# Routing operands in the unused half of the state's PSUM bank, the first expert's low parts subtracted on GpSimd, and x stored one chunk later

## The chip, the cores and the metric

The kernel runs on one core of a Trainium2 chip. Five engines work beside each other: TensorE (PE, with its weight load PEld), VectorE (DVE), ScalarE (ACT), GpSimd (POOL) and SyncE (SP), which here only issues transfers. Each engine takes its instructions in order. The metric is the device time of one execution in microseconds (us); lower is better.

## What is computed

A retention-like attention layer (B = 4 batches, 8 heads, 768 tokens, head size 64) feeds a mixture of 8 experts with two experts for each token.

```python
for t in range(S):
    state = gamma * state + einsum('bhd,bhe->bhde', k[:, :, t], v[:, :, t])
    y[:, :, t] = scale * einsum('bhd,bhde->bhe', q[:, :, t], state)
x = y.transpose(0, 2, 1, 3).reshape(B * S, H * D)            # 3072 x 512
noisy = x @ w_gate + log1p(exp(x @ w_noise)) * noise
top2 = argpartition(-noisy, 2, axis=1)[:, :2]
top2_w = softmax of the two                                 # with + 1e-9
for e in range(8):
    for k in range(2):
        mask = top2[:, k] == e
        h = maximum(x[mask] @ w1[e], 0)
        out[mask] += top2_w[mask, k, None] * (h @ w2[e])
```

## The kernel before

**Stages.** A loop over 24 chunks of 128 tokens (`for j in range(NCH)`, L672; six chunks, NC, make a batch) runs from the start to about 142 us: attention for chunk j, and in the same iterations the routing of batches that are complete and the preparation of the first expert's weights. From about 142 to 220 us the routing of the last batch and the token lists of all experts are finished while the first expert's products begin. From 220 to 690 us the eight experts run on TensorE.

**One iteration.** The order in which the code stands is the order on each engine. Iteration j has, in this order: `qk(j+1)` (L312: 16 products of k with the scaled q of the next chunk, into pA); `v_scale(j+1)` and `q_scale(j+2)` on GpSimd (L285, L291); loads for chunk j+4 on SP; `x_total(j-1)` (PE L348, sum of squares into XSS) and `x_hi(j-1)` (DVE L157 and L158 read XSS and make a power of two, `upx`; ACT L353 writes the fp16 high part of x); `masked(j+1)` (DVE L319); `x_lo(j-1)` (DVE L357, the low part); what the table `between` has for j; `y_mm(j)` (PE L326 and L329 into pY, ACT L334 squares it, PE L339 adds k v into the state's bank pU, ACT L345 copies the state to U in SBUF); `x_rows(j-2)` (PE L363 transposes, ACT L365 copies to `xr`, SP stores it to HBM, L366); `logits(j-2)` (PE L373 and L376 into PL); and at last what the table `todo` has for j. pU is written in columns 0 to 63 of each of its four 128-column parts; in the last chunk of a batch there is no state product. The buffers of `qs` number 3, of `vp`, `am` and pA 2 each, of pY 2.

**The routing.** When a batch is complete, its route steps run in the iterations that follow, with n the last iteration of the batch: `route_a` at n+2 (DVE L386 to L391 on the logits, ACT L394 and L395 Exp and Ln), `route_b` n+3 (L403 to L412: noise and the two best), `route_b2` and `route_c` n+4 (L419 one-hot rows, L422, L441, L442), `places` n+5 (PE L432, places within the experts, into POS), `route_d` n+5 (L465 to L487), `route_e` n+6 and n+7 (L498 and L500, 12 instructions each), `route_w` n+8 (gates), `table` n+8 (PE L506 into LST) and `route_f`. After batch 1 (iteration 19) three gathers of rows follow on GpSimd (L608). The routing of batches 0, 1 and 2 runs in iterations 7 to 13, 13 to 19 and 19 to 23.

**The first expert's weights.** Each of its two matrices comes in four pieces of 128x1024 fp32: `w_load` (SP), `w_sum` (ACT L181, sum of squares), `w_scale` (PE L184 into SUM, DVE: a power of two), `w_hi` (ACT L202, fp16 of the scaled piece), `w_lo` (DVE L207, scaled piece minus its high part, one instruction). The tables at L649 to L656 say in which iteration each stands. The other seven experts' weights are prepared in the stages behind, with the same functions.

**Banks and waits.** PSUM has eight banks here: pA (2), pY (2), pX, pU, pR and pL. Waits between engines are kept for each of these tiles as a whole: an engine that touches a tile waits for what another engine did with that tile before, whichever columns it was. XSS lies in pL beside the logits PL; POS, LST and SUM lie in pR.

Of the kernel before, what the change touches and what calls it, by code (L numbers as in the profile page):

```python
# [94 lines left out]
def moe_kernel(ctx, tc, qT, kT, kt, vt, noise, wgn, w1, w2, ctab, qtab, xbuf, gbuf, out):  # L95
# [35 lines left out]
    lanes = consts.tile([128, 128], F16, name="lanes")  # L131
    blks = consts.tile([128, NCOL], F16, name="blks")
# [6 lines left out]
    invx = consts.tile([128, NCH], F32, name="invx")  # L139
# [139 lines left out]
    VP, AM, QS, PY, X, SS = {}, {}, {}, {}, {}, {}  # L279
    pU = psum.tile([128, HP, 128], F32, name="pU")  # L280
# [78 lines left out]
    def x_rows(j):  # L359
# [6 lines left out]
        nc.sync.dma_start(xbuf[128 + j * C:128 + (j + 1) * C, :], xr)  # L366
# [13 lines left out]
    cum = work.tile([128, NL], F32, name="cum")  # L380
    nc.vector.memset(cum, 0.0)
    R["cum"] = cum

    def route_a(b):
        sl = slice(b * NC, (b + 1) * NC)
        nc.vector.tensor_scalar(invx[:, sl].bitcast(I32), upx[:, sl].bitcast(I32), -1.0, float(254 << 23),  # L386
# [637 lines left out]
```

## Time and profile before

| | |
|---|---|
| time, median of 3 runs (lowest, highest) | 705.52 us (703.36, 708.82) |
| profiled execution: its own time, its span | 706.42 us, 704.6 us |
| mean granted TensorE clock of that span | 0.972 |
| TensorE busy | 661.5 us (94%) |
| TensorE's weight load busy | 401.2 us (57%) |
| VectorE busy | 296.4 us (42%) |
| ScalarE busy | 315.0 us (45%) |
| GpSimd busy | 266.1 us (38%) |

The profile is of one execution. Its span is what the trace covers; the execution's own time is 706.42 - 704.6 = 1.8 us longer. Instructions are named by engine, line of the code, operation and tiles (`pL L373` is the instruction of line 373 that writes tile pL). "Busy" counts time in which an engine executes; overlapping instructions of a pipelined engine are counted once in a window. "PEclk" is the granted TensorE clock as a share of full speed (1.00 is 2.4 GHz, 0.50 is 1.2 GHz).

### The profile page before, as it was taken

Reading aid. Unit: us, or ns where it says so; the run is one execution under the profiler, and the core shown is the slowest. Engines: PE = TensorE matmul, PEld = TensorE weight load, DVE = VectorE, ACT = ScalarE, POOL = GpSimd, SP = SyncE. Lnnn points to the kernel's source line nnn. Section 1 sums busy time; section 2 is a strip of 40 time slices with the busy share of each in tenths; the row PEclk is TensorE's granted clock in tenths of the full one; section 3 lists DMA queues with packets and bytes.
Section 4 is the critical chain, followed back from the end, with each engine's and each line's share of the span. In section 5 each row is a group of like instructions: output and inputs, shape, how many; then the busy total and the mean of one; then the engine's idle time right before and its main releaser. Section 6 shows DMA issues by size and latency. Waiting matters only on the chain. (4 is left out here: it accounts for less than half of the span.)

```text
span 704.6 us, 12916 instructions
## 1 busy us (share of the span) xinstructions
PE 661.5 (94%) x5165; PEld 401.2 (57%) x5165; DVE 296.4 (42%) x800; ACT 315.0 (45%) x560; POOL 266.1 (38%) x214
## 2 busy tenths in 40 slices
PE   8997886989799999999999999999999999999992
PEld 5886775754576554555455545554654565455540
DVE  4678997868024534352215321522252144215100
ACT  5777673631135643444434443544453444344110
POOL 4543343311532503461436143614352333335021
PEclk9998997999999999999999999999999999999996
DMA  9997899432794444764667266726572674472032
GB/s 335 315 401 270 272 398 367 106 90 55 240 219 76 136 150 82 129 173 147 99 124 220 83 120 125 257 41 117 107 265 52 130 190 152 76 133 34 12 48 32
DMA packets 95230, 112.36 MB, mean 159 GB/s; under 512 B 62208, under 2 KB 62464, under 8 KB 91584
## 3 DMA queue, kind: packets, MB, share of 16 engines
q1 hardware_dynamic: 81472, 84.03, 39.2%
q0 software_dynamic: 13120, 26.63, 19.9%
q8 instruction: 42, 0.69, 0.4%
q10 hardware_dynamic: 576, 0.84, 0.4%
q14 instruction: 20, 0.16, 0.1%
HBM read 72.03 MB, written 26.34 MB: 140 GB/s over the span
## 5 line engine op out<-in xcount | busy, mean ns | idle before, releaser
L751 POOL DMA_INDIRECT out<-ot,idx x54 | 88.2, 1633 | 279.3 <-ACT ot L746 161.8
L721 PE MATMUL pH<-xe,w1h 128*128 128x384 f16 (+4 forms) x544 | 177.1, 326 | 5.3 <-DVE hl L725 3.9
L723 PE MATMUL pH<-xe,w1l 128*128 128x384 f16 (+4 forms) x544 | 177.1, 326 | 0.0
L722 PE MATMUL pH<-xe,w1h 128*128 128x384 f16 (+4 forms) x544 | 177.0, 325 | 0.0
L725 DVE SCALAR_TENSOR_TENSOR hl<-pH,hh 128x384 f16<-128x384 f32 (+4 forms) x136 | 74.4, 549 | 218.0 <-ACT hh L724 196.4
L762 PE MATMUL pO<-w2h,hl 128*128 128x512 f16 x384 | 146.3, 381 | 0.0
L760 PE MATMUL pO<-w2h,hh 128*128 128x512 f16 x384 | 146.2, 381 | 0.0
L761 PE MATMUL pO<-w2l,hh 128*128 128x512 f16 x384 | 146.1, 381 | 0.0
L724 ACT ACTIVATE hh<-pH 128x384 f16<-128x384 f32 (+4 forms) x136 | 65.5, 484 | 132.9 <-PE pH L723 123.8
L746 ACT ACTIVATE ot<-pO,gse 128x512 f32<-128x512 f32 (+4 forms) x54 | 37.1, 687 | 178.3 <-PE pO L762 163.9
L207 DVE SCALAR_TENSOR_TENSOR w1l<-wst,wsc,w1h 128x1024 f16<-128x1024 f32 x32 | 41.8, 1316 | 102.1 <-ACT w1h L202 102.1
L618 POOL DMA_INDIRECT gx<-gbuf,idx x54 | 69.6, 1290 | 23.2 <-issue 15.6
L608 POOL DMA_INDIRECT xg<-xbuf,idx x55 | 54.3, 986 | 58.7 <-DVE key L531 17.7
L722 PEld LDWEIGHTS <-w1h 128*128 128x128 f16 x544 | 53.7, 99 | 38.3 <-issue 5.6
L721 PEld LDWEIGHTS <-w1h 128*128 128x128 f16 x544 | 54.3, 100 | 34.1 <-issue 1.4
L723 PEld LDWEIGHTS <-w1l 128*128 128x128 f16 x544 | 53.7, 99 | 34.5 <-issue 0.7
L181 ACT ACTIVATE junk<-wst 128x1024 bf16<-128x1024 f32 x64 | 67.0, 1048 | 0.1
L762 PEld LDWEIGHTS <-hl 128*128 128x128 f16 x384 | 37.6, 98 | 45.8 <-issue 0.8
L760 PEld LDWEIGHTS <-hh 128*128 128x128 f16 x384 | 38.3, 100 | 44.5 <-issue 0.7
L761 PEld LDWEIGHTS <-hh 128*128 128x128 f16 x384 | 37.7, 98 | 44.5 <-issue 0.8
L285 POOL TENSOR_TENSOR vp<-in_v,ct 128x512 f32<-128x512 f32 x24 | 25.2, 1048 | 58.2 <-issue 26.1
L207 DVE SCALAR_TENSOR_TENSOR w2l<-wst,wsc,w2h 128x1024 f16<-128x1024 f32 x32 | 40.8, 1275 | 0.0
(163 smaller groups left out, 745.1 us busy)
## 6 DMA issues: line engine op xcount, KB each, us to landing
wst<-w SPq DMA_DIRECT2D x28, 1024.0 KB
in_q<-qT SPq DMA_DIRECT2D x24, 256.0 KB
in_k<-kT SPq DMA_DIRECT2D x24, 256.0 KB
in_v<-vt SPq DMA_DIRECT2D x24, 256.0 KB
xbuf<-xr SPq DMA_DIRECT2D x24, 256.0 KB
out<-zero SPq DMA_DIRECT2D x6, 1024.0 KB
in_kt<-kt SPq DMA_DIRECT2D x20, 256.0 KB
wst<-w SPq DMA_DIRECT2D x8, 512.0 KB
```

Source lines behind the costliest of these rows:

```text
L181: nc.scalar.activation(junk, st[:, i * 1024:(i + 1) * 1024], AF.Square, accum_out=ss[:, i:i + 1])
L207: nc.vector.scalar_tensor_tensor(lo, st[:, i * 1024:(i + 1) * 1024], sc[:, 0:1], hi, op0=OP.mult, op1=OP.subtract)
L618: nc.gpsimd.indirect_dma_start(out=GX[e][:, t, :], out_offset=None, in_=gbuf[:128 + rows], in_offset=bass.IndirectOffsetOnAxis(ap=idx[:, i ...
L721: nc.tensor.matmul(p[:, :n], whi, xh, start=(k == 0), stop=False)
L722: nc.tensor.matmul(p[:, :n], whi, xl, start=False, stop=False)
L723: nc.tensor.matmul(p[:, :n], wlo, xh, start=False, stop=(k == KT - 1))
L724: nc.scalar.activation(hh[:, f, n0:n1], p[:, :n], AF.Relu)
L725: nc.vector.scalar_tensor_tensor(hl[:, f, n0:n1], p[:, :n], 0.0, hh[:, f, n0:n1], op0=OP.max, op1=OP.subtract)
L751: nc.gpsimd.indirect_dma_start(out=out, out_offset=bass.IndirectOffsetOnAxis(ap=idx[:n, i:i + 1], axis=0), in_=ot[:n], in_offset=None, com ...
L760: nc.tensor.matmul(p, a, WT["2h"][:, f, :], start=(f == 0), stop=False)
L761: nc.tensor.matmul(p, a, WT["2l"][:, f, :], start=False, stop=False)
L762: nc.tensor.matmul(p, c, WT["2h"][:, f, :], start=False, stop=(f == FT - 1))
```

## The change

Four things change.

1. The banks: XSS moves from pL to pR and lies there beside SUM; POS and LST move from pR to pL beside the logits PL.
2. Operands of VectorE's routing instructions that lay in SBUF now lie in columns 64 to 127 of the four parts of pU, the state's bank: the constant rows `lanes` and `blks` (for L498, L500) and `lidx` (copied there by four more instructions in iteration 2), `invx`, the running count `cum`, the noise products and gates (`small`), and one wide scratch row (`wide`). Two steps gain an instruction: `route_b2` makes three one-hot rows in place of two, and `route_c` copies `cum`; `route_w` adds the two gates with a reduction in place of an addition.
3. The first expert's low parts are made by `w_lo_pool`: ScalarE scales the piece in place (128x1024, fp32), and GpSimd subtracts the high part. The steps of this expert stand two or three iterations later than before: of the first matrix, loads in iterations 4 to 8 (before 2 to 6), sums 6 to 10 (4 to 8), the scale in 11 (9), high parts 11 and 12 (9 and 10), low parts 11, 12, 13 and 14 (9, 10, 10 and 11); of the second, loads 11 to 15 (8 to 12), sums 13 to 17 (10 to 14), the scale in 18 (16), high parts 18 and 19 (16 and 17), low parts 18, 19, 20 and 21 (17, 18, 19 and 21). The stores of zeros to `out` (`zero_out`) move from iterations 13 to 19 to iterations 18 to 22.
4. `x_store(j-3)`, the store of a chunk's `xr` to HBM, stands in iteration j behind the loads; before, chunk j-2 was stored in iteration j right behind its copy.

```diff
-    lanes = consts.tile([128, 128], F16, name="lanes")
-    blks = consts.tile([128, NCOL], F16, name="blks")
+    lanes16 = consts.tile([128, 128], F16, name="lanes16")
+    blks16 = consts.tile([128, NCOL], F16, name="blks16")
...
-    invx = consts.tile([128, NCH], F32, name="invx")
...
     PL = pL[:, 0:NC * 4 * E].rearrange("p (c s e) -> p c s e", c=NC, s=2)
-    XSS = pL[:, NC * 4 * E:NC * 4 * E + 4]
-    POS = pR[:, 96:96 + (NC + 1) * NL].rearrange("p (c e) -> p c e", c=NC + 1)
-    LST = pR[:, 168:168 + NCOL]
-    SUM = pR[:, 480:488]
+    XSS = pR[:, 0:4]
+    SUM = pR[:, 8:16]
+    POS = pL[:, 200:200 + (NC + 1) * NL].rearrange("p (c e) -> p c e", c=NC + 1)
+    LST = pL[:, 280:280 + NCOL]
+    pU = psum.tile([128, HP, 128], F32, name="pU")
+
+    lanes = pU[:, 0, 64:128].bitcast(F16)
+    blks = pU[:, 1, 64:64 + NCOL // 2].bitcast(F16)
+    lidx = pU[:, 1, 92:92 + NL], pU[:, 1, 102:102 + NL]
+    cump = pU[:, 1, 112:112 + NL]
+    small = pU[:, 2, 64:112]
+    invp = [pU[:, 2, 112 + i * NC:112 + (i + 1) * NC] for i in range(2)]
+    wide = pU[:, 3, 64:64 + NC * NL].rearrange("p (c e) -> p c e", c=NC)
 
...
+    def w_lo_pool(e, which, i):
+        st, ss, sc = ST[which, e]
+        hi, lo = w_parts(which, i)
+        s = st[:, i * 1024:(i + 1) * 1024]
+        nc.scalar.activation(s, s, AF.Copy, scale=sc[:, 0:1])
+        nc.gpsimd.tensor_tensor(lo, s, hi, op=OP.subtract)
 
...
         nc.scalar.activation(xr, pX.rearrange("p a c -> p (a c)"), AF.Copy)
-        nc.sync.dma_start(xbuf[128 + j * C:128 + (j + 1) * C, :], xr)
+        XR[j] = xr
+
+    def x_store(j):
+        nc.sync.dma_start(xbuf[128 + j * C:128 + (j + 1) * C, :], XR.pop(j))
 
...
     def route_a(b):
         sl = slice(b * NC, (b + 1) * NC)
-        nc.vector.tensor_scalar(invx[:, sl].bitcast(I32), upx[:, sl].bitcast(I32), -1.0, float(254 << 23),
+        nc.vector.tensor_scalar(invp[b % 2].bitcast(I32), upx[:, sl].bitcast(I32), -1.0, float(254 << 23),
                                 op0=OP.mult, op1=OP.add)
         lg = work.tile([128, NC, 2 * E], F32, name="lg")
         nc.vector.tensor_copy(lg, PL[:, :, 1])
         nc.vector.tensor_tensor(lg, lg, PL[:, :, 0], op=OP.add)
-        nc.vector.scalar_tensor_tensor(lg, lg, gx, invx[:, b * NC:(b + 1) * NC, None].to_broadcast([128, NC, 2 * E]),
+        nc.vector.scalar_tensor_tensor(lg, lg, gx, invp[b % 2][:, :, None].to_broadcast([128, NC, 2 * E]),
                                        op0=OP.mult, op1=OP.mult)
         sp = work.tile([128, NC, E], F32, name="sp")
         nc.scalar.activation(sp, lg[:, :, E:], AF.Exp)
-        nc.scalar.activation(sp, sp, AF.Ln, bias=1.0)
-        R[b] = (lg, sp)
+        nc.scalar.activation(small.rearrange("p (c e) -> p c e", c=NC), sp, AF.Ln, bias=1.0)
+        R[b] = lg
 
     def route_b(b):
 
-        lg, sp = R[b]
+        lg, sp = R[b], small.rearrange("p (c e) -> p c e", c=NC)
         o = int(b >= B0)
         ny = work.tile([128, NC, NY], F32, name="ny")
         nc.vector.tensor_tensor(sp, sp, nz[:, b * NC:(b + 1) * NC, :], op=OP.mult)
...
     def route_b2(b):
         oh, m8, i8 = R[b]
         s3 = [128, NC, NL]
-        for k in range(2):
-            nc.vector.tensor_tensor(oh[:, k], K("lidx3" if b == B - 1 else "lidx")[:, None, :].to_broadcast(s3),
+        for o, k in ((oh[:, 0], 0), (wide, 1), (oh[:, 1], 1)):
+            nc.vector.tensor_tensor(o, lidx[b == B - 1][:, None, :].to_broadcast(s3),
                                     i8[:, :, k:k + 1].to_broadcast(s3), op=OP.is_equal)
         mb = work.tile([128, NC, NL], BF, name="mb")
-        nc.vector.tensor_tensor(mb, oh[:, 0], oh[:, 1], op=OP.add)
+        nc.vector.tensor_tensor(mb, wide, oh[:, 0], op=OP.add)
         den = work.tile([128, NC], F32, name="den", bufs=B)
         nc.vector.tensor_tensor(den, m8[:, :, 1], m8[:, :, 0], op=OP.subtract)
         nc.scalar.activation(den, den, AF.Exp)
...
     def route_c(b):
         oh, mb, den = R[b]
-        cb = work.tile([128, 2, NL], F32, name="cb")
-        nc.vector.tensor_scalar(cb[:, 0], R["cum"], -1.0, float(CAP), op0=OP.mult, op1=OP.add)
-        nc.vector.tensor_tensor(cb[:, 1], K("base"), R["cum"], op=OP.add)
+        cb = work.tile([128, 3, NL], F32, name="cb")
+        nc.vector.tensor_scalar(cb[:, 0], cump, -1.0, float(CAP), op0=OP.mult, op1=OP.add)
+        nc.vector.tensor_tensor(cb[:, 1], cump, K("base"), op=OP.add)
+        nc.vector.tensor_copy(cb[:, 2], cump)
         R[b] = (oh, den, cb)
 
...
-        nc.vector.tensor_scalar(dn, den, 1.0, 1e-9, op0=OP.add, op1=OP.add)
-        nc.vector.reciprocal(dn, dn)
-        nc.vector.tensor_tensor(g[:, 0], dn, invx[:, sl], op=OP.mult)
-        nc.vector.tensor_tensor(g[:, 1], den, g[:, 0], op=OP.mult)
+        nc.vector.tensor_scalar(small[:, 12:12 + NC], den, 1.0, 1e-9, op0=OP.add, op1=OP.add)
+        nc.vector.reciprocal(dn, small[:, 12:12 + NC])
+        g = small[:, :2 * NC].rearrange("p (k c) -> p k c", k=2)
+        nc.vector.tensor_tensor(g[:, 0], invp[b % 2], dn, op=OP.mult)
+        nc.vector.tensor_tensor(g[:, 1], g[:, 0], den, op=OP.mult)
         t = work.tile([128, 2, NC, NL], F32, name="t")
-        nc.vector.tensor_tensor(t, oh, g[:, :, :, None].to_broadcast([128, 2, NC, NL]), op=OP.mult)
-        nc.vector.tensor_tensor(gateb[:, sl], t[:, 0], t[:, 1], op=OP.add)
+        nc.vector.tensor_tensor(t, g[:, :, :, None].to_broadcast([128, 2, NC, NL]), oh, op=OP.mult)
+        nc.vector.tensor_reduce(gateb[:, sl], t.rearrange("p k c e -> p c e k"), axis=AX.X, op=OP.add)
...
-        nc.vector.tensor_tensor(ov, POS[:, :NC, :], cb[:, 0:1, :].to_broadcast(s3), op=OP.is_ge)
+        nc.vector.tensor_tensor(wide, POS[:, :NC, :], cb[:, 0:1, :].to_broadcast(s3), op=OP.is_ge)
         nc.vector.tensor_tensor(sl, POS[:, :NC, :], cb[:, 1:2, :].to_broadcast(s3), op=OP.add)
         ps = work.tile(s3, F32, name="ps", bufs=B)
-        nc.vector.tensor_tensor(ps, POS[:, :NC, :], R["cum"][:, None, :].to_broadcast(s3), op=OP.add)
-        nc.vector.scalar_tensor_tensor(ov, ov, BIG, sl, op0=OP.mult, op1=OP.add)
-        cn = work.tile([128, NL], F32, name="cum")
-        nc.vector.tensor_tensor(cn, POS[:, NC, :], R["cum"], op=OP.add)
+        nc.vector.tensor_tensor(ps, POS[:, :NC, :], cb[:, 2:3, :].to_broadcast(s3), op=OP.add)
+        nc.vector.scalar_tensor_tensor(wide, wide, BIG, sl, op0=OP.mult, op1=OP.add)
+        nc.vector.tensor_tensor(cump, POS[:, NC, :], cb[:, 2], op=OP.add)
...
-        at((9, 10, 10, 11)[i], w_lo, 0, "1", i)
...
+        at((11, 12, 13, 14)[i], w_lo_pool, 0, "1", i)
...
+        if j >= 3:
+            x_store(j - 3)
```

On GpSimd, around iterations 9 to 14 (`vp` and `qs` are the scaled v and q of a chunk, `w1l` a low part), the program before has

```order
L285 TENSOR_TENSOR vp_1005<-in_v_739,ct_83 128x512
L291 TENSOR_TENSOR qs_1007<-in_q_810,gq_119 128x512
L285 TENSOR_TENSOR vp_1114<-in_v_823,ct_83 128x512
L291 TENSOR_TENSOR qs_1116<-in_q_911,gq_119 128x512
L285 TENSOR_TENSOR vp_1198<-in_v_924,ct_83 128x512
L291 TENSOR_TENSOR qs_1200<-in_q_1009,gq_119 128x512
```

and nothing between these. In the changed program there stands, for the same chunks,

```order
L299 TENSOR_TENSOR vp_993<-in_v_738,ct_83 128x512
L305 TENSOR_TENSOR qs_995<-in_q_810,gq_119 128x512
L299 TENSOR_TENSOR vp_1093<-in_v_823,ct_83 128x512
L305 TENSOR_TENSOR qs_1095<-in_q_907,gq_119 128x512
L223 TENSOR_TENSOR w1l_109<-wst1_564,w1h_108 128x1024
L299 TENSOR_TENSOR vp_1189<-in_v_920,ct_83 128x512
L305 TENSOR_TENSOR qs_1191<-in_q_997,gq_119 128x512
L223 TENSOR_TENSOR w1l_109<-wst1_564,w1h_108 128x1024
L299 TENSOR_TENSOR vp_1279<-in_v_1010,ct_83 128x512
L305 TENSOR_TENSOR qs_1281<-in_q_1097,gq_119 128x512
```

A subtraction now stands ahead of the scaling of the next chunk's v and of the q of the chunk behind that; the first pair behind a subtraction is `vp` of chunk 13 and `qs` of chunk 14, the next `vp` of chunk 14 and `qs` of chunk 15. Each subtraction waits for ScalarE.

On ScalarE, in iteration 11 (`xr` is the copy of transposed x, L379 in the changed code), the changed program has, with the waits in brackets,

```order
L379 ACTIVATE xr<-pX 128x1024 [waits DMAHW6_49,PE_49]
L210 ACTIVATE w1h<-wst_564,wsc_566 128x1024 [waits DVE_49]
L222 ACTIVATE wst_564<-wst_564,wsc_566 128x1024 [waits Activation_49]
L210 ACTIVATE w1h<-wst_564,wsc_566 128x1024
L367 ACTIVATE x_1201<-pY,upx 128x512 [waits DVE_49]
```

The row of L222, the scaling in place on which the subtraction waits, is new there; the rows of L210 are those of L202 before.

On VectorE, where `route_a` of batch 0 stands (iteration 7), the program before has

```order
L357 SCALAR_TENSOR_TENSOR x_734<-pY,upx,x_734 128x512 [waits Activation_49]
L386 TENSOR_SCALAR invx<-upx 128x6
L389 COPY lg<-pL 128x96 [waits PE_49]
L390 TENSOR_TENSOR lg<-lg,pL 128x96 [waits DVE_49]
L391 SCALAR_TENSOR_TENSOR lg<-lg,gx,invx 128x96 [waits DVE_49]
L157 TENSOR_SCALAR p2m<-pL 128x1 [waits PE_49]
```

and the changed program

```order
L371 SCALAR_TENSOR_TENSOR x_733<-pY,upx,x_733 128x512 [waits Activation_49]
L403 TENSOR_SCALAR pU<-upx 128x6 [waits PE_49,Activation_49]
L406 COPY lg<-pL 128x96 [waits PE_49]
L407 TENSOR_TENSOR lg<-lg,pL 128x96 [waits DVE_49]
L408 SCALAR_TENSOR_TENSOR lg<-lg,gx,pU 128x96 [waits DVE_49]
L165 TENSOR_SCALAR p2m<-pR 128x1 [waits PE_49]
```

The first instruction of the step now writes pU and waits there for TensorE's state products and ScalarE's copies of the same iteration, and the read of XSS at the end (L157 before, L165 now) is of pR in place of pL.

## Rows read from the trace of the kernel before

**Rows 1.** Busy time of each engine in each stage (start and end, length in us, then TensorE, its weight load, VectorE, ScalarE, GpSimd with their counts of instructions, the granted clock, the share of the DMA engines and GB/s).

```profile
54.00:142.00 88.00, 71.77 (x998) 62.71 (x997) 78.47 (x255) 54.04 (x102) 34.06 (x31) 0.90 0.83 279
142.00:220.00 78.00, 70.74 (x470) 44.28 (x470) 32.40 (x160) 19.88 (x44) 22.23 (x20) 0.93 0.59 147
220.00:690.00 470.00, 468.25 (x2997) 252.66 (x2996) 151.82 (x285) 202.58 (x326) 181.96 (x136) 1.00 0.53 121
```

**Rows 2.** The waits of TensorE from 54 to 142 us (engine, tile and line that waited, what it waited for: us in total, times, longest).

```profile
PE pL L373 <- DVE p2m L157: 6.1, 2, 3.3
PE pL L348 <- DVE lg L390: 3.9, 2, 2.7
PE pR L432 <- DVE mb L422: 1.2, 1, 1.2
PE pR L506 <- DVE a L500: 1.0, 5, 0.3
```

**Rows 3.** Busy time of each engine in three stretches in which the granted clock was at its lower level (columns as in the first group).

```profile
64.90:71.30 6.40, 4.56 (x41) 4.25 (x42) 6.37 (x19) 3.22 (x6) 0.00 (x0) 0.50 0.38 124
109.40:116.00 6.60, 6.19 (x48) 4.98 (x45) 6.46 (x24) 1.72 (x3) 0.44 (x1) 0.50 1.05 402
122.90:126.30 3.40, 3.40 (x40) 3.03 (x39) 3.37 (x7) 2.27 (x7) 1.04 (x2) 0.50 0.48 107
```

**Rows 4.** The timeline of TensorE at 26 to 39 us, in iterations without a route step (start, duration in us, the work): the start of the products of q and k of chunks 5, 6, 7 and 8, and the first state products.

```profile
26.34 1.16 PE L312 MATMUL pA<-qs,in_k 64*128 64x128 f32 x16
29.65 0.69 PE L339 MATMUL pU<-vp,in_kt 128*64 128x64 f32 x16
31.00 1.16 PE L312 MATMUL pA<-qs,in_k 64*128 64x128 f32 x16
34.95 1.16 PE L312 MATMUL pA<-qs,in_k 64*128 64x128 f32 x16
38.38 0.83 PE L312 MATMUL pA<-qs,in_k 64*128 64x128 f32 x10
```

**Rows 5.** The timeline of ScalarE behind the first of those.

```profile
29.82 0.60 ACT L334 ACTIVATE junk<-pY 128x512 bf16<-128x512 f32 x1 [1.10 <-PE pY L329]
30.31 0.20 ACT L334 ACTIVATION_READ_ACCUMULATOR junk<-pY 128x1 bf16 x1
30.40 0.76 ACT L345 ACTIVATE U<-pU 64x256 f32<-64x256 f32 x2
31.18 1.02 ACT L365 ACTIVATE xr<-pX 128x1024 f16<-128x1024 f16 x1
```

**Rows 6.** VectorE's groups of instructions by line and shape from 54 to 142 us, while GpSimd scales q and v (count | busy us, mean ns of one | idle before).

```profile
L500 DVE TENSOR_SCALAR a<-lanes,lf 128x128 f16<-128x128 f16 x30 | 9.2, 308 | 0.0
L207 DVE SCALAR_TENSOR_TENSOR w1l<-wst,wsc,w1h 128x1024 f16<-128x1024 f32 x4 | 6.1, 1547 | 3.1 <-ACT w1h L202 3.1
L207 DVE SCALAR_TENSOR_TENSOR w2l<-wst,wsc,w2h 128x1024 f16<-128x1024 f32 x4 | 5.1, 1273 | 0.0
L405 DVE TENSOR_TENSOR ny<-sp,lg 128x48 f32<-128x48 f32 x2 | 2.4, 1197 | 0.0
L419 DVE TENSOR_TENSOR oh<-ct,i 128x60 f32<-128x60 f32 x4 | 2.3, 613 | 0.0
```

**Rows 7.** The same view from 148 to 168 us, where GpSimd scales nothing.

```profile
L500 DVE TENSOR_SCALAR a<-lanes,lf 128x128 f16<-128x128 f16 x12 | 3.0, 247 | 0.0
L419 DVE TENSOR_TENSOR oh<-ct,i 128x60 f32<-128x60 f32 x2 | 0.3, 216 | 0.0
L405 DVE TENSOR_TENSOR ny<-sp,lg 128x48 f32<-128x48 f32 x1 | 0.2, 209 | 0.0
```

**Rows 8.** GpSimd's groups by line and shape from 54 to 142 us (the last is the gathers behind iteration 19).

```profile
L291 POOL TENSOR_TENSOR qs<-in_q,gq 128x512 f32<-128x512 f32 x12 | 15.3, 1272 | 4.9 <-DMA in_q<-qT 4.9
L285 POOL TENSOR_TENSOR vp<-in_v,ct 128x512 f32<-128x512 f32 x13 | 13.6, 1049 | 38.0 <-issue 23.7 <-PE pU L339 12.1 <-DMA in_q<-qT 1.1
L608 POOL DMA_INDIRECT xg<-xbuf,idx x3 | 3.1, 1029 | 7.1 <-DVE dn L451 6.5 <-PE pL L376 0.3 <-issue 0.3
```

**Rows 9.** ScalarE's groups by line and shape from 54 to 142 us.

```profile
L202 ACT ACTIVATE w1h<-wst,wsc 128x1024 f16<-128x1024 f32 x4 | 4.4, 1137 | 0.0
L181 ACT ACTIVATE junk<-wst 128x1024 bf16<-128x1024 f32 x4 | 4.2, 1051 | 0.0
L181 ACT ACTIVATION_READ_ACCUMULATOR junk<-wst 128x1 f32 x4 | 0.8, 196 | 0.0
L394 ACT ACTIVATE sp<-lg 128x48 f32<-128x48 f32 x2 | 0.5, 243 | 3.7 <-DVE lg L391 3.7
```

**Rows 10.** The timeline of VectorE around the first half of `route_e` (12 instructions from 68.02 us, then a low part), and around `route_a` (its first and last instruction) and `route_w` (the same) of a batch in the quiet stage behind 142 us.

```profile
68.02 0.29 DVE L498 TENSOR_SCALAR bb<-blks,lf,ct 128x56 f16<-128x56 f16 x1
...
70.22 1.28 DVE L207 SCALAR_TENSOR_TENSOR w1l<-wst,wsc,w1h 128x1024 f16<-128x1024 f32 x1
...
149.19 0.16 DVE L386 TENSOR_SCALAR invx<-upx 128x6 int32<-128x6 int32 x1
...
149.84 0.32 DVE L391 SCALAR_TENSOR_TENSOR lg<-lg,gx,invx 128x96 f32<-128x96 f32 x1
...
160.51 0.16 DVE L451 TENSOR_SCALAR dn<-den 128x6 f32<-128x6 f32 x1
...
161.65 0.22 DVE L457 TENSOR_TENSOR gateb<-t 128x60 f32<-128x60 f32 x1
```

More of the change, by code (lines that the diff above doesn't have):

```diff
@@ L277, in moe_kernel @@
         U.append(u)
-    VP, AM, QS, PY, X, SS = {}, {}, {}, {}, {}, {}
-    pU = psum.tile([128, HP, 128], F32, name="pU")
+    VP, AM, QS, PY, X, SS, XR = {}, {}, {}, {}, {}, {}, {}
     def v_scale(j):
@@ L379, in moe_kernel @@
     R = {}
-    cum = work.tile([128, NL], F32, name="cum")
-    nc.vector.memset(cum, 0.0)
+    cum = consts.tile([128, NL], F32, name="cum")
+    nc.vector.memset(cump, 0.0)
     R["cum"] = cum
@@ L474, in route_d @@
         if b == B - 2:
-            nc.vector.tensor_scalar(cn[:, E + 1:NL], cn[:, E:E + 1], float(SECOND), None, op0=OP.max)
-        R["cum"] = cn
+            nc.vector.tensor_scalar(cump[:, E + 1:NL], cump[:, E:E + 1], float(SECOND), None, op0=OP.max)
         t = work.tile([128, 2, NC, NL], F32, name="t")
-        nc.vector.tensor_tensor(t, oh, ov[:, None].to_broadcast([128, 2, NC, NL]), op=OP.mult)
-        sf = work.tile([128, 2, NC], F32, name="sf")
+        nc.vector.tensor_tensor(t, wide[:, None].to_broadcast([128, 2, NC, NL]), oh, op=OP.mult)
@@ L480, in route_d @@
+        sf = small[:, :2 * NC].rearrange("p (k c) -> p k c", k=2)
+        si = small[:, 2 * NC:4 * NC].bitcast(I32)
+        lb = small[:, 4 * NC:].bitcast(I32)
         nc.vector.tensor_reduce(sf, t, axis=AX.X, op=OP.add)
-        si = work.tile([128, 2, NC], I32, name="si")
-        nc.vector.tensor_copy(si, sf)
-        lb = work.tile([128, 2, 2, NC], I32, name="lb")
-        nc.vector.tensor_scalar(lb[:, 0], si, 127, None, op0=OP.bitwise_and)
-        nc.vector.tensor_scalar(lb[:, 1], si, 7, None, op0=OP.arith_shift_right)
+        nc.vector.tensor_copy(si, small[:, :2 * NC])
@@ L526, in ranks @@
     def ranks():
+        nc.vector.tensor_copy(cum, cump)
         m = E - 1
@@ L648, in moe_kernel @@
     for i in range(4):
-        at((2, 3, 5, 6)[i], w_load, 0, "1", i)
-        at((4, 5, 7, 8)[i], w_sum, 0, "1", i)
-        at((9, 9, 10, 10)[i], w_hi, 0, "1", i)
-        at((9, 10, 10, 11)[i], w_lo, 0, "1", i)
-        at((8, 9, 11, 12)[i], w_load, 0, "2", i)
-        at((10, 11, 13, 14)[i], w_sum, 0, "2", i)
-        at(16 + i // 2, w_hi, 0, "2", i)
-        at((17, 18, 19, 21)[i], w_lo, 0, "2", i)
-    for i in range(7):
-        at(13 + i, zero_out, i)
-    at(2, nc.vector.tensor_copy, lanes, K("lanes"))
-    at(2, nc.vector.tensor_copy, blks, K("blks"))
-    between.setdefault(9, []).append((w_scale, 0, "1"))
-    between.setdefault(16, []).append((w_scale, 0, "2"))
+        at((4, 5, 7, 8)[i], w_load, 0, "1", i)
+        at((6, 7, 9, 10)[i], w_sum, 0, "1", i)
+        at(11 + i // 2, w_hi, 0, "1", i)
+        at((11, 12, 13, 14)[i], w_lo_pool, 0, "1", i)
+        at((11, 12, 14, 15)[i], w_load, 0, "2", i)
+        at((13, 14, 16, 17)[i], w_sum, 0, "2", i)
+        at(18 + i // 2, w_hi, 0, "2", i)
+        at((18, 19, 20, 21)[i], w_lo_pool, 0, "2", i)
+    for i in range(7):
+        at((18, 19, 20, 20, 21, 21, 22)[i], zero_out, i)
+    at(2, nc.vector.tensor_copy, lanes16, K("lanes"))
+    at(2, nc.vector.tensor_copy, blks16, K("blks"))
+    at(2, nc.vector.tensor_copy, lanes.bitcast(F32), lanes16.bitcast(F32))
+    at(2, nc.vector.tensor_copy, blks.bitcast(F32), blks16.bitcast(F32))
+    at(2, nc.vector.tensor_copy, lidx[0], K("lidx"))
+    at(2, nc.vector.tensor_copy, lidx[1], K("lidx3"))
+    between.setdefault(11, []).append((w_scale, 0, "1"))
+    between.setdefault(18, []).append((w_scale, 0, "2"))
     mid = SECOND // 128
@@ L701, in moe_kernel @@
     x_lo(NCH - 1)
+    x_store(NCH - 3)
     x_rows(NCH - 2)
     logits(NCH - 2)
+    x_store(NCH - 2)
     lctx.close()
@@ L808, in moe_kernel @@
     logits(NCH - 1)
+    x_store(NCH - 1)
     for t in range(3, mid + 1):
```

8 lines of the change are left out of this document (4 added, 4 removed).

## The prediction

> **What bounds the kernel now.** I read the stages first [rows 1]. From 220 to 690 us TensorE is busy 468.25 of 470 us at full clock: nothing that the change touches lies there. From 54 to 142 us TensorE is busy only 71.77 of 88, so 16.2 us are idle, at a mean granted clock of 0.90, while VectorE is busy 78.47 of 88. This loop is where the change acts. What TensorE waits for in it is in the view of waits [rows 2]: L373 on VectorE's read of XSS (L157), 6.1 us; L348 on VectorE's read of the logits (L390), 3.9; L432 and L506 on route steps, 1.2 and 1.0. Sum 12.2. The first two are waits for a tile: XSS and the logits share pL, so the products of one wait until VectorE, late with its list, has read the other. Behind the waits the granted clock is at its lower level, 1.2 GHz, for 6.4 + 6.6 + 3.4 = 16.4 us [rows 3]; work there takes twice its time, so about 8.2 us are lost to the clock.
>
> **The change, part by part.**
>
> *Banks.* XSS and logits no longer share a tile, so the waits of L373 and L348 go: -10.0. In their place the logits wait for VectorE's reads of POS and LST, which now lie in pL: twice for each batch, between 0 and the 3.3 of L373's longest [rows 2]. Those reads stand a whole chunk, 4.7 us [rows 4], ahead of the logits behind them, and VectorE is relieved (below), so I take 0; without that cover it is up to 6 x 3.3.
>
> *VectorE's load.* Eight low parts leave it, 6.1 + 5.1 = 11.2 us [rows 6]. Route instructions whose two inputs lie in SBUF are longer while GpSimd scales q and v: L405 takes 1197 ns against 209 in the stage where GpSimd scales nothing, L419 613 against 216, L500 308 against 247 [rows 6, 7]. If an operand in pU gives back the quiet duration, that is 2 x 0.988 + 4 x 0.397 + 30 x 0.061 = 5.4 us. The bounds are 0 and 5.4; I take 5.4. The few added instructions (a third one-hot row, a copy) are of the kind of L419, 0.2 us in the quiet stage, beside 17 us of relief. With VectorE early, the waits of L432 and L506 go as well: -2.2. All four waits gone make -12.2.
>
> The Trainium skill, "SBUF — State Buffer", section "Who interferes with whom", says that a VectorE instruction with two SBUF inputs is blocked by a GpSimd instruction that reads SBUF, and one with at most one SBUF input is not. By that rule the whole 5.4 us come back; the trace agrees so far as L405 and L419 are several times longer beside GpSimd, but none of before has an operand moved.
>
> *Clock.* If no long wait is left, the 8.2 us come back too. What follows brings other long waits, so I count a clock loss of the same size there: -8.2 and +8.2.
>
> *Low parts on GpSimd.* No row has the subtraction. Nearest are GpSimd's scalings of 128x512, `vp` 1.05 us and `qs` 1.27 [rows 8]; twice the elements give 2.1 to 2.5, and I take 2.3 (one input is fp16, the other fp32, both full). ScalarE's scaling in place is as `w1h` or L181, 1.05 to 1.14 us [rows 9]. Eight of each add 9 us to ScalarE, which was busy 54.04 of 88, and 18 us to GpSimd, busy 34.06 of 88 [rows 1]. Neither is full. But GpSimd takes its work in order, and the subtraction stands ahead of the next `vp` and of the `qs` of the chunk behind that. What counts is when ScalarE gets to the scaling.
>
> The Trainium skill, "GPSIMD Engine Reference", section 3.1 (Elementwise), measured a GpSimd `tensor_tensor` of 2048 fp32 at 4497 ns, 1.96 times VectorE's, and advises VectorE for such work: an estimate of 2.25 us for 1024. It speaks against this part; by it the sum would be the same within 0.1 us for each subtraction, and no run here shows it yet.
>
> First stall. Count from the start of the products of q and k in iteration 11. The square of y starts 29.82 - 26.34 = 3.48 later, and takes 0.60 + 0.20: 4.3 [rows 4, 5]. Iteration 11 has no state product; the copy `xr` ends at 5.3, one `w1h` at 6.4, the scaling at 7.5 [rows 5, 9]. Subtraction 9.8, `vp` 10.85, `qs` of chunk 14 at 12.1 [rows 8]. Undisturbed, TensorE wants it after a last chunk (31.00 to 34.95, 3.95) and a first chunk (34.95 to 38.38, 3.43): 7.4 [rows 4]. **Stall 12.1 - 7.4 = 4.7.**
>
> Second stall, for `qs` of chunk 16, counted from the products of chunk 14: square done 4.3, state copies 5.1 [rows 5]. In this iteration `route_w` (160.51 to 161.87, 1.36) and `route_a` (149.19 to 150.16, 0.97) stand ahead of Exp [rows 10]: 7.4; Exp and Ln 0.24 each, 7.9; a sum of squares 1.05 + 0.20, 9.1; the scaling 10.2 [rows 9]; subtraction 12.5, `vp` and `qs` 14.8. Wanted after two chunks of 31.00 - 26.34 = 4.66: 9.3 [rows 4]. **Stall 5.5.**
>
> Third stall, in iterations 18 to 21: three gathers of 1.03, a subtraction and a pair, 3.1 + 2.3 + 2.3 = 7.7, behind a token list that comes not before 5.1 (as the state copies do), are done at 12.8 [rows 5, 8]: 3.5 behind 9.3. Bounds 0 and, with `qs` behind two subtractions, 5.8. **I take 3.5.** These three are +13.7.
>
> *Weights' totals.* SUM now shares pR with XSS; L184's product waits for VectorE's read of it. Bounds twice 0 and twice 3.3 [rows 2]; I take 0.75 each, as VectorE is relieved: +1.5.
>
> *State's bank.* Each route step now waits for the state products and copies of its iteration, and the next state products wait for the step. The copies end at 30.40 + 0.76, 1.5 us behind the start of the products at 29.65; of 4.66 us that leaves 3.1 [rows 4, 5]. The longest steps, half of `route_e` (68.02 to 70.22, 2.2) and `route_w` with `route_a` (2.3), fit [rows 10]. If VectorE is more than 0.8 us late they don't; in some 14 iterations with both, bounds 0 and 14 x 0.8 = 11. I take 2: the cover is VectorE's relief.
>
> *Stores of x, zeros, loads.* SP issues the stores behind the loads in place of behind a ScalarE copy; a load there waits less. Nothing on TensorE's list waits for them [rows 2], cover the DMA engines' 17% of idle share [rows 1]: 0. In 142 to 220 us VectorE is busy 32.40 of 78: its added instructions are hidden, 0.
>
> **Sum.** -12.2 - 8.2 + 8.2 + 13.7 + 1.5 + 2 = +5.0. Against the profiled execution, 706.4 us, that is 711.4. This execution lies 0.9 above the median of the runs, 705.5; on that it would be 710.5. I say 711.
>
> **The rivals.**
>
> *Relief prevails (faster).* For it speaks that all four waits named go, and that they are sure. It needs the third stall to be hidden, and the clock to stay at its higher level through stalls of about 5 us: -12.2 - 8.2 + 4.7 + 5.5 = -10.2, 696 us; with half of the clock given back 700. It decides if the two stalls together stay under about 12 and the lower clock under 8 us. Against it: waits of 3.3 and 2.7 were long enough before for the stretches at the lower clock to lie behind them [rows 2, 3].
>
> *The state's bank becomes a ring.* VectorE, TensorE and ScalarE pass pU round in every chunk of iterations 7 to 23. At 0.8 us in each of 14 iterations the sum is +5 - 2 + 11 = +14: 720. From 0.4 us in each on (5.6 in all) it is above 1%. For it: the window of 3.1 leaves 0.8 only. Against: VectorE loses 17 of 78 us.
>
> The Trainium skill, "PSUM — Partial Sum Buffer", section "PSUM bank collisions raise a hardware error", holds that engines must be kept apart by bank and quadrant, not by columns, which is why the free half of the bank is not free in time.
>
> *The operands in pU shorten nothing.* If what makes L405 and L419 long is not where their inputs lie, VectorE keeps 5.4 us, and the waits of L432 and L506 stay: +5 + 2.2 = 713.6.
>
> **How the numbers follow.** Chances: forecast 0.50 (its own range 705 to 719, from a third stall of 0 to 5.8, subtractions of 2.1 to 2.5, L184 of 0 to 6.6), relief 0.22, ring 0.16, nothing shortened 0.12. A measurement of this kernel can tell about 1%, 7 us: 698.5 and 712.6. Faster takes most of relief, 0.20. Slower takes the ring, some 0.2 of the forecast above 712.6 and a third of the last: 0.40. The rest is 0.40. The range from 699 to 720 leaves out half of relief and the end of the ring, not quite 2 in 10.
>
> **What would show it.** In the changed profile L373 and L348 should have no long wait; L405 and L419 should be near 0.2 us; L312 should wait for `qs` from GpSimd in three places of 3 to 6 us, with the lower clock behind them; the subtraction should take 2.1 to 2.5 us and ScalarE's scaling 1.1. The loop should end at 147 in place of 142 us, and the experts take the same 470. If L312 never waits for `qs`, the forecast is wrong toward faster; if L339 waits for VectorE in most chunks, toward slower.

## The result and the profile after

The changed kernel takes 711.39 us (median of 9 runs, 708.49 to 717.24), the kernel before 705.52 (now 9 runs, 701.39 to 708.82). The ratio is 1.010, with a 95% interval from 1.0061 to 1.0139: slower by about 1% (the medians are 5.9 us apart). The profiled execution is the fastest of the nine: 708.49 us, a span of 706.6, so that the two profiles differ by 2.0 us only, 1.6 of them in the loop. Left out below are the four times that lie over 1.5% above the fastest of their kernel: 1706 us once in the run of the banks alone, 1705 and 775 us in the repeat of the kernel before (which therefore has no ratio), and 710.87 us in the first of the last four runs.

The stages of the changed kernel (columns as in [rows 1]):

```profile
54.00:142.00 88.00, 67.24 (x975) 59.42 (x973) 60.48 (x252) 62.83 (x113) 49.14 (x38) 0.92 0.79 256
142.00:220.00 78.00, 69.26 (x466) 42.88 (x466) 35.01 (x167) 20.12 (x43) 21.71 (x20) 0.93 0.58 161
220.00:690.00 470.00, 468.38 (x3001) 252.93 (x2999) 152.29 (x289) 203.23 (x327) 176.21 (x136) 1.00 0.52 121
```

In the loop VectorE is busy 18 us less than in [rows 1], ScalarE 9 and GpSimd 15 more, and TensorE is idle for 20.8 us in place of 16.2. The experts are as they were. TensorE's waits from 54 to 142 us, which answer to [rows 2]:

```profile
PE pA L326 <- POOL qs L305: 10.7, 3, 4.9
PE pR L192 <- DVE p2m L165: 3.4, 2, 1.9
PE pA L326 <- DVE m L427: 3.3, 1, 3.3
PE pR L362 <- ACT junk L348: 1.0, 1, 1.0
...
PE pL L521 <- DVE a L515: 0.6, 3, 0.2
```

The waits of the logits for x's sums, of x's sums for the logits and of `places` are gone, and the one for the list rows is 0.6 in place of 1.0. In their place stand waits of the products of q and k (L326, L312 before) for the scaled q (L305). Where the first of them ends, GpSimd's and TensorE's timelines read

```profile
66.75 2.12 POOL L223 TENSOR_TENSOR w1l<-wst,w1h 128x1024 f16<-128x1024 f32 x1 [7.42 <-ACT wst L222]
68.83 1.04 POOL L299 TENSOR_TENSOR vp<-in_v,ct 128x512 f32<-128x512 f32 x1
69.84 1.26 POOL L305 TENSOR_TENSOR qs<-in_q,gq 128x512 f32<-128x512 f32 x1
```

```profile
71.15 1.93 PE L326 MATMUL pA<-qs,in_k 64*128 64x128 f32 x16 [4.33 <-POOL qs L305]
...
87.36 2.15 PE L326 MATMUL pA<-qs,in_k 64*128 64x128 f32 x16 [4.88 <-POOL qs L305]
...
117.04 1.16 PE L326 MATMUL pA<-qs,in_k 64*128 64x128 f32 x16 [1.48 <-POOL qs L305]
...
125.62 1.79 PE L326 MATMUL pA<-qs,in_k 64*128 64x128 f32 x16 [3.28 <-DVE m L427]
```

GpSimd idles 7.42 us for ScalarE's scaling, then subtraction, `vp` and `qs` follow without a gap, and TensorE starts when `qs` is done, 69.84 + 1.26 = 71.10. The last of the four is put down to VectorE's L427, on which these products do not depend; GpSimd's row of that time does:

```profile
124.30 1.26 POOL L305 TENSOR_TENSOR qs<-in_q,gq 128x512 f32<-128x512 f32 x1
```

It ends at 125.56, 0.06 before TensorE starts, so this wait too is for the scaled q. The four waits stand at chunks 14, 16, 21 and 22 and make 4.33 + 4.88 + 1.48 + 3.28 = 14.0 us. Behind them the granted clock falls again to its lower level for a while:

```profile
71.80:75.50 3.70, 3.70 (x43) 3.23 (x40) 2.50 (x8) 2.51 (x3) 3.70 (x3) 0.58 0.21 81
86.00:92.20 6.20, 4.84 (x37) 4.27 (x38) 2.72 (x12) 2.49 (x4) 5.62 (x5) 0.52 1.05 406
126.00:129.40 3.40, 3.40 (x33) 2.83 (x30) 2.57 (x16) 1.68 (x2) 2.33 (x2) 0.52 1.35 213
```

VectorE's groups in the loop show what the operands in the state's bank do:

```profile
L513 DVE TENSOR_SCALAR bb<-pU,lf,ct 128x56 f16<-128x56 f16 x27 | 8.1, 299 | 0.9 <-ACT U L359 0.9
L515 DVE TENSOR_SCALAR a<-pU,lf 128x128 f16<-128x128 f16 x26 | 7.2, 275 | 0.0
L436 DVE TENSOR_TENSOR oh<-pU,i 128x60 f32<-128x60 f32 x4 | 0.9, 220 | 4.8 <-ACT U L359 4.7
L422 DVE TENSOR_TENSOR ny<-pU,lg 128x48 f32<-128x48 f32 x2 | 0.4, 208 | 0.0
```

L422 (L405 before) takes 208 ns and L436 (L419 before) 220, as in the quiet stage of [rows 7]; L515 (L500 before) takes 275, more than the quiet 247. An instruction whose two inputs stayed in SBUF is still held: `den` (L441) takes 0.94 us at 94.97, while GpSimd scales q from 94.62 to 95.88, and 0.16 us at 132.71, where GpSimd does nothing.

### The profile page after: what moved, and what is told of

It reads as the page before. It is cut to its first block, busy times and chain, and to the rows that moved or that the text cites. A ratio compares the mean times of both kernels' runs of the same rounds, so it can differ in the third digit from the quotient of the medians.

```text
span 706.6 us, 12960 instructions
## 1 busy us (share of the span) xinstructions
PE 658.0 (93%) x5165; PEld 398.2 (56%) x5165; DVE 281.3 (40%) x805; ACT 323.8 (46%) x568; POOL 277.1 (39%) x222
## 5 line engine op out<-in xcount | busy, mean ns | idle before, releaser
L634 POOL DMA_INDIRECT gx<-gbuf,idx x54 | 66.2, 1226 | 23.5 <-issue 14.3
L215 DVE SCALAR_TENSOR_TENSOR w1l<-wst,wsc,w1h 128x1024 f16<-128x1024 f32 x28 | 35.7, 1284 | 99.0 <-ACT w1h L210 99.0
L326 PE MATMUL pA<-qs,in_k 64*128 64x128 f32 x384 | 31.0, 302 | 15.9 <-POOL qs L305 12.6
```

The source lines that it names most:

```text
L634: nc.gpsimd.indirect_dma_start(out=GX[e][:, t, :], out_offset=None, in_=gbuf[:128 + rows], in_offset=bass.IndirectOffsetOnAxis(ap=idx[:, i ...
```

## The experiments

The twelve runs fell on three chips, whose times of the kernel before have medians of 695.06 us (first four), 695.4 (next four) and 707.78 (last four). So ratios to the kernel before on the same chip are compared; the expectations in microseconds were written for a kernel before of 705.5 us. An interval of 95% stands behind each ratio.

**Which part costs: low parts back on VectorE, and subtractions behind the scalings.** The first run:

```diff
-        at((11, 12, 13, 14)[i], w_lo_pool, 0, "1", i)
+        at((11, 12, 13, 14)[i], w_lo, 0, "1", i)
-        at((18, 19, 20, 21)[i], w_lo_pool, 0, "2", i)
+        at((18, 19, 20, 21)[i], w_lo, 0, "2", i)
```

> The changed kernel with the eight low parts of the first expert given back to VectorE (one instruction each, in the iterations where GpSimd's subtraction stood; ScalarE's scaling in place is gone). Theory 1 (the subtractions hold up the scaled q, three stalls of about 14 us in the changed kernel and the lower clock behind them, while the banks and operands gain): no wait of TensorE for the scaled q after 54 us, VectorE busier by 8 x 1.3 = 10 us, time 695 to 702, faster than before by 4 to 10. Rival, the ring through the state's bank: the route steps' waits stay, time 709 to 713, as the changed kernel.

Measured: 1.0016 (0.9995 to 1.0036). The change's loss goes, but the gain of 4 to 10 us over the kernel before does not come. In the second run ScalarE's scaling stays, and `w_sub`, GpSimd's subtraction alone, is put in `between` of the next iteration:

```diff
+    for i in range(4):
+        between.setdefault((12, 13, 14, 15)[i], []).append((w_sub, 0, "1", i))
+        between.setdefault((19, 20, 21, 22)[i], []).append((w_sub, 0, "2", i))
```

> The changed kernel with each GpSimd subtraction moved into the next iteration, behind the scalings of v and q that stand there; nothing else moves, and all work stays. Theory 1: the stalls of 4.3, 4.9 and 4.8 us for the scaled q go, and about 6 us of lower clock with them: 711.4 - 14 - 6 = 691, up to 698 where other waits come in their place. Rival, the ring: no change, 709 to 713. Rival, GpSimd or ScalarE simply has too much work: the wait for the scaled q comes back one chunk later, 705 to 711.

Measured: 1.0031 (1.0013 to 1.0048). All the work is there in another order, and some 0.7% comes back. So it is GpSimd's order that costs, much more than the amount of its work: with the low parts on VectorE, on the same chip, the ratio is only 0.15% lower. But of the 14 us of stalls and the clock behind them only about 5 us come back. Its waits from 54 to 147 us show part of the rest:

```profile
PE pL L525 <- DVE a L519: 5.1, 14, 1.8
PE pR L192 <- DVE p2m L165: 3.4, 2, 1.9
PE pR L366 <- ACT junk L352: 3.0, 3, 1.5
PE pA L330 <- POOL qs L309: 2.4, 1, 2.4
```

With TensorE earlier, the list rows (L519), the weights' total (L192), the squares of y (L352) and once the scaled q are late.

Another part is lost behind the loop. The experts' first product starts at 136.54 us in the first run and at 137.23 in the second, against 138.19 in the run of the banks alone (the next one, on the same chip, as fast as the kernel before). From there to the end of the span these three take 559.0, 558.9 and 554.2 us. The first 20 us of the experts in each (columns as in [rows 1]):

```profile
136.54:156.54 20.00, 17.25 (x109) 9.54 (x106) 10.31 (x59) 5.35 (x11) 1.89 (x2) 0.78 0.46 154
137.23:157.23 20.00, 16.31 (x110) 9.34 (x107) 11.74 (x68) 5.52 (x11) 1.88 (x2) 0.83 0.42 140
138.19:158.19 20.00, 18.28 (x130) 10.83 (x127) 13.70 (x79) 6.39 (x13) 1.88 (x2) 0.91 0.29 80
```

The granted clock is 0.78 and 0.83 there, in place of 0.91: over 20 us that is 2.6 and 1.6 us of the 4.8 and 4.7 us by which the two are longer. Where the others go was not traced.

**The banks alone, on the kernel before.**

```diff
-    XSS = pL[:, NC * 4 * E:NC * 4 * E + 4]
+    XSS = pR[:, 0:4]
+    SUM = pR[:, 8:16]
...
+    POS = pL[:, 200:200 + (NC + 1) * NL].rearrange("p (c e) -> p c e", c=NC + 1)
+    LST = pL[:, 280:280 + NCOL]
```

> The kernel before with the banks alone exchanged (sums of squares of x and of the weights in one, places and lists beside the logits), all else as before. Theory 1: the waits of L373 and L348 (6.1 and 3.9 us) go, but VectorE stays as late as it was, so some of them come back at products that need its masked scores: 698 to 704, faster by 2 to 8. Rival, that these waits only show VectorE's lateness: 704 to 708, the same sum of waits at other lines.

Measured: 1.001 (0.9985 to 1.0034). No gain shows, and one of 2 to 8 us is excluded. At its wait of 3.3 us TensorE's timeline of the kernel before reads

```profile
58.63 1.53 PE L312 MATMUL pA<-qs,in_k 64*128 64x128 f32 x16
...
66.11 0.19 PE L373 MATMUL pL<-wg,x 128*128 128x32 f16 x1 [3.28 <-DVE p2m L157]
...
67.10 2.53 PE L312 MATMUL pA<-qs,in_k 64*128 64x128 f32 x16 [0.63 <-DVE am L319]
```

In this run TensorE's and VectorE's timelines read, at the same place,

```profile
58.67 1.53 PE L312 MATMUL pA<-qs,in_k 64*128 64x128 f32 x16
...
67.14 1.15 PE L312 MATMUL pA<-qs,in_k 64*128 64x128 f32 x6 [4.10 <-DVE am L319]
```

```profile
62.48 3.55 DVE L207 SCALAR_TENSOR_TENSOR w1l<-wst,wsc,w1h 128x1024 f16<-128x1024 f32 x2
65.95 0.14 DVE L157 TENSOR_SCALAR p2m<-pR 128x1 int32<-128x1 int32 x1
66.13 0.15 DVE L158 TENSOR_SCALAR upx<-p2m 128x1 int32<-128x1 int32 x1
66.20 1.28 DVE L319 TENSOR_TENSOR am<-pA,ct 128x512 f32<-128x512 f32 x2
```

Two low parts hold VectorE for 3.5 us. With the shared bank the logits wait for the read of x's sum behind them; without it the products of q and k wait for the masked scores (`am`) behind that, 4.10 us, for they need one of the two tiles. The two products of q and k are 8.47 us apart in both kernels. The rival of the expectation is what happened.

**The subtractions alone, on the kernel before** (the function `w_lo_pool`, and the first expert's and `zero_out`'s iterations of the change).

> The kernel before with the low parts as ScalarE's scaling and GpSimd's subtraction alone, and the first expert's steps and the stores of zeros in the iterations of the changed kernel; banks and operands as before. Theory 1: the three stalls are added, VectorE's relief takes part of L373's waits away: 711 to 720. Rival, that the relief of VectorE is what counts and banks and operands cost: 698 to 705.

Measured: 1.0094 (1.0064 to 1.0125). That is as much as the whole loss of the change, without its banks and operands. Its waits from 54 to 147 us:

```profile
PE pA L319 <- POOL qs L298: 6.3, 2, 3.4
PE pA L319 <- DVE a L507: 4.3, 1, 4.3
...
PE pA L319 <- DVE neg L530: 1.5, 1, 1.5
PE pL L380 <- DVE p2m L157: 0.8, 1, 0.8
PE pL L355 <- DVE lg L397: 0.8, 1, 0.8
```

The waits of 4.3 and 1.5 us end 0.06 and 0.05 us behind a scaling of q on GpSimd (at 70.85 and 119.81 us), so 12.1 us are waits for the scaled q. The last two lines are the waits that were at L373 and L348 in [rows 2]: 1.6 us in place of 10.0, although x's sums and the logits still share their bank. With the low parts gone from VectorE and their steps later, the shared bank costs little.

**Both kernels once more, on the chip of the next two runs.** No edit.

> The kernel before once more, unchanged, for a profile on the chip on which these experiments run. Ratio 1.00 within 0.003; the waits of L373 and L348 on VectorE as before, some 10 us, and the first product of the experts at about 142 us. A rival, that this chip's loop runs otherwise than in the first profile: these waits would be elsewhere.

> The changed kernel once more, unchanged, beside the others. Ratio 1.006 to 1.014, as measured first; the waits for the scaled q 10 to 14 us in the loop after 54 us. If the ratio is near 1.00 the difference depended on the chip.

The profiled execution of the kernel before took 694.9 us, and its wait of L373 was again 6.1 us, but that of L348 for the logits was not there. The changed kernel: 1.0134 (1.0100 to 1.0167), with waits for the scaled q as in the first profile (10.7 in three, and one of 2.3 put down to L427). The first product of the experts starts at 139.98 and at 146.41 us, a loop longer by 6.4; in the first pair of profiles it was 142.41 and 143.98.

**List rows from SBUF, and the weights' totals in another bank.** Both stand on the kernel with the subtractions behind the scalings.

```diff
-            nc.vector.tensor_scalar(bb[:, k, c, :], blks, lf[:, 1, k, c:c + 1], K("tokv")[:, j:j + 1],
+            nc.vector.tensor_scalar(bb[:, k, c, :], blks16, lf[:, 1, k, c:c + 1], K("tokv")[:, j:j + 1],
...
-            nc.vector.tensor_scalar(a[:, k, c, :], lanes, lf[:, 0, k, c:c + 1], None, op0=OP.is_equal)
+            nc.vector.tensor_scalar(a[:, k, c, :], lanes16, lf[:, 0, k, c:c + 1], None, op0=OP.is_equal)
```

> The changed kernel with the subtractions behind the scalings of the next iteration (as tried before), and with the constant rows of the twelve instructions a half that make the lists read from SBUF in place of the state's bank. Theory now: these instructions waited for ScalarE's copies of the state, late by its scaling, and TensorE's list products waited for them (3.3 us at 70 us, some 5 to 8 in all with the lower clock behind); without that wait the ratio to before is 0.990 to 0.997, where the subtractions moved alone gave 1.003. Rival, that VectorE's operands in PSUM are needed for speed: the instructions take 0.31 to 0.33 us in place of 0.28 to 0.30, and the ratio stays at 1.002 to 1.006.

Measured: 1.0067 (1.0041 to 1.0093). My theory fell: it is not faster, and by its ratio rather slower than with the rows in the bank (1.0031, on another chip). The rival named the cause, but the mean of L519 is 423 ns, above the 0.31 to 0.33 us expected. VectorE's and GpSimd's timelines of this run:

```profile
70.43 1.32 DVE L519 TENSOR_SCALAR a<-lanes,lf 128x128 f16<-128x128 f16 x1
...
71.88 0.24 DVE L519 TENSOR_SCALAR a<-lanes,lf 128x128 f16<-128x128 f16 x1
...
72.25 2.21 DVE L519 TENSOR_SCALAR a<-lanes,lf 128x128 f16<-128x128 f16 x1
```

```profile
70.44 1.27 POOL L309 TENSOR_TENSOR qs<-in_q,gq 128x512 f32<-128x512 f32 x1
72.27 2.13 POOL L227 TENSOR_TENSOR w1l<-wst,w1h 128x1024 f16<-128x1024 f32 x1 [0.56 <-ACT wst L222]
```

An instruction of 0.24 us that starts beside a GpSimd instruction of 1.27 or 2.13 us takes 1.32 or 2.21: it lasts until GpSimd's is done. With its row in the state's bank each of the 24 takes 0.27 or 0.28 in the loop of the kernel with the subtractions behind the scalings. So the operands in the bank are of use, beside GpSimd. The prediction cited the Trainium skill, "SBUF — State Buffer", section "Who interferes with whom", for instructions with two SBUF inputs, and counted this one among them. It has a single row of data, and what bears on it there is a condition that the prediction left out: an instruction with one SBUF input is free of GpSimd only outside the two-port modes, a `tensor_scalar` can run in one, and then the second to issue waits for the whole of the first. That it runs in such a mode here no run shows; the 2.21 beside 2.13 us agree.

The next run adds

```diff
-    SUM = pR[:, 8:16]
+    SUM = pL[:, 340:348]
```

> As the last, and the totals of the weights' squares moved from the bank of x's sums to the one of the logits. Theory: the two waits of the weights' total for VectorE (1.5 and 1.9 us) go, ratio lower by another 0.003 to 0.005, 0.986 to 0.993. Rival: VectorE is what is late, and TensorE waits the same 3.4 us for its masked scores or its lists one instruction later; ratio as the last.

Measured: 1.0018 (0.9997 to 1.0039), 0.5% below the run before it on the same chip. The two waits of the totals for the read of x's sum, 3.1 us in the run before it, are gone; 1.7 us, for ScalarE's sum of squares, are left at that line. So the weights' total in the bank of x's sums is a real cost, shown on the kernel with the subtractions behind the scalings.

**What beats the kernel before.** Low parts on VectorE as in the first run, with the totals moved:

> The changed kernel with the low parts on VectorE (as tried first, ratio 1.0016) and the totals of the weights' squares in the bank of the logits. Theory: banks and operands do gain in the loop, but two waits of 1.5 and 1.9 us for x's sums in the weights' bank gave that back; ratio 0.995 to 0.998. Rival, that they gain nothing since VectorE's list is as late as before: 1.000 to 1.003.

Measured: 0.9904 (0.9873 to 0.9936), faster than the kernel before and than expected; the changed kernel itself was not run on this chip. The first product of the experts starts at 133.51 us. The size of this gain is less sure than the interval says: the lowest times of the two kernels, 700.34 and 702.01 us, are only 0.24% apart, and the mean granted clock of their runs is 0.976 against 0.972, so part of it may lie in how often the clock falls. The subtractions behind the scalings, with the totals moved:

> The changed kernel with the subtractions behind the next scalings (ratio 1.0031) and the totals in the bank of the logits, rows of the lists left in the state's bank. If both effects add (-0.005 for the totals, -0.0036 for the rows in the state's bank, as the two kernels with the rows in SBUF had 1.0067 and 1.0018): 0.997 to 0.999. Rival: once the totals don't wait, the lists do; 1.001 to 1.003.

Measured: 0.9942 (0.9917 to 0.9967), faster than expected. Then one high part in each iteration:

```diff
-        at(11 + i // 2, w_hi, 0, "1", i)
+        at(11 + i, w_hi, 0, "1", i)
...
-        at(18 + i // 2, w_hi, 0, "2", i)
+        at(18 + i, w_hi, 0, "2", i)
```

> As the last, with one high part in each of four iterations in place of two in each of two. Theory: in iteration 11 ScalarE does high part, scaling, high part in a row (3.4 us) before the next chunk's x and square, and the state's copies and with them VectorE's list rows are late by that; with one high part less there 1.1 us of it go: ratio 0.994 to 0.998, wait for the list rows shorter than in the last. Rival, ScalarE's order doesn't matter: as the last.

Measured: 0.9971 (0.9939 to 1.0003). The wait for list rows falls from 4.6 to 2.6 us, but one for the scaled q rises from 0.9 to 2.6, and no gain shows. The last run is the first of these last four with the old iterations of the weights' steps and of `zero_out`:

> The first of these four with the first expert's steps and the stores of zeros in the iterations of the kernel before: only banks, operands and the later store of x are changed. Theory, the iterations themselves make little: within 0.003 of the first of these four. Rival, the later iterations were needed because VectorE's low parts meet the route steps: 0.004 or more above it.

Measured: 0.9991 (0.9965 to 1.0018), as the rival had it. Banks (with the totals moved), operands and the later store alone gain nothing that shows; with the weights' steps two or three iterations later, and the stores of zeros later too, the same kernel gains 0.9%. TensorE's timeline of this last run has, at the place discussed,

```profile
59.33 1.61 PE L326 MATMUL pA<-qs,in_k 64*128 64x128 f32 x16 [0.57 <-DMA in_q<-qT]
...
67.69 1.68 PE L326 MATMUL pA<-qs,in_k 64*128 64x128 f32 x10 [3.90 <-DVE am L333]
```

They start 8.36 us apart, where the kernel before has 8.47; in the first of the four, the same two start at 57.06 and 62.41, since the low parts no longer stand beside `route_d` there.

## Why the prediction was right, and where it was not

The time (711.0 against 711.39) and the direction came out as forecast. The first two stalls came at the chunks that were named, with nearly the sizes that were worked out. The loop, forecast 5 us longer, is 1.6 us longer in the first pair of profiles and 6.4 in the second. By the steps of the prediction:

- **The banks' waits (-10.0), `places` and the lists (-2.2).** They are gone in the changed kernel, but for 0.6 us. Their cause is the step that failed: "The first two are waits for a tile: XSS and the logits share pL". The tile only decided which product waited. VectorE's two low parts made it late, and without the shared bank the wait is 4.10 us at the masked scores; with the low parts elsewhere and the bank still shared, 1.6 of the 10.0 us are left. Alone, the banks gain nothing that shows (ratio 1.001), nor do they with the operands in the old iterations (0.9991).
- **VectorE's relief.** L405 and L419 fell to the quiet durations as taken; L500 fell to 275 ns, not 247: 2 x 0.989 + 4 x 0.393 + 30 x 0.033 = 4.5 us in place of 5.4.
- **Low parts on GpSimd.** The subtraction takes 2.13 us (2.3 taken, bounds 2.1 to 2.5), the scaling 1.14. The stalls are 4.33 (4.7 forecast), 4.88 (5.5) and, behind the gathers, 3.28 (3.5); one of 1.48 at chunk 21, behind the first subtraction of the second matrix, was not forecast. Together they are 14.0 against 13.7. The third came near by luck: counted from the products of chunk 20 at 108.97 us, the gathers start at 8.5 us and not at 5.1, and the scaled q is wanted at 13.4 and not at 9.3. That the subtractions cause the loss is shown: the same work in another order takes off about 0.7%, and the subtractions alone, on the kernel before, cost 0.94%.
- **Weights' totals (+1.5).** They wait 3.4 us. Moved to the other bank, the ratio fell by 0.5% on one chip; across chips, 1.0016 to 0.9904 and 1.0031 to 0.9942, by more.
- **State's bank (+2).** No wait of the state products for VectorE stands among those after. VectorE waits for ScalarE's copies (4.7 us before L436), but TensorE's waits for VectorE's lists are 0.6 us. The ring did not decide.
- **Clock.** Nearly as assumed in the first pair of profiles: stretches of 13.3 us together in the loop with a granted clock of 0.52 to 0.58, where [rows 3] have 16.4 at 0.50. In the second pair the mean from 54 us to the experts' first product is 0.85 after and 0.88 before.

The sum held, but not its parts, and that the time came out within 0.4 us is in part luck. The 20.4 us of gains were booked to banks, operands and the clock behind their waits. But with banks and operands the change loses 1.00% (1.34% on the second chip), and the subtractions without them 0.94%: the waits of L373 and L348 end with the low parts' move, not with the shared bank. What the prediction set against each other as gains of one part and losses of another both come from that move, with a net of +6.6 us (0.0094 x 705.5), clock and relief of VectorE included. The 6.8 us (0.0096 x 705.5) that the first of the last four runs gains need the later iterations; whether banks and operands have a share in them no run shows.

A wait of several us on one engine covers what is late on the others; taken away, the next one stands there. So the rival "relief prevails", 696 to 700, needed more than the stalls' absence: without them the ratio was 1.0016 or 1.0031, not 0.985.

Three things stay open. The later store of x, the zeros' later iterations and the weights' later iterations (low parts on VectorE, banks as before) were not tried by themselves. The first and the last four runs were on chips whose kernel before differs by 12 us; how much of the 0.9 to 1.1% that the moved totals brought across chips is due to that was not settled (0.5% on one chip). And why a kernel whose loop ends earlier took some 5 us longer behind it is explained only in part, by the granted clock.

## To carry to other kernels

An in-order engine that feeds the critical path should get a long instruction with a late input only behind the short ones that the path needs next: here one iteration's place gave back 0.7%, and the other engine 0.8%. A wait that names a shared tile tells where the late engine was met, not that the tile is the cause; look at what the late engine did just before, and at which product would meet it next. Take away the wait's supposed cause alone, before you book its microseconds to it. Terms of a sum that are waits of the same engine cannot be added as if each were free to be cashed alone.

## What the runs showed that I had not expected

A VectorE `tensor_scalar` with one fp16 row of data in SBUF can be held for a whole GpSimd instruction (0.24 to 2.21 us beside 2.13); the mean of [rows 6], 308 ns against 247, hid this: two of those thirty took 1.28 and 1.12 us, beside a scaling of q and one of v. The same instruction with its row in PSUM takes 275 ns in the loop and behind it, so it is the slower one where GpSimd is quiet.
